# Loading q, k, v and the weights through GpSimd's DMA queue, with x turned on TensorE for three of four batches

## The chip, the cores and the metric

The program runs on one core of a Trainium2 chip. The metric is the device time of one execution, in microseconds (us); smaller is better. The engines are TensorE (PE: matmuls; PEld: its weight loads), VectorE (DVE), ScalarE (ACT), GpSimd (POOL) and SyncE (SP, which here only issues DMAs). [...]

## The reference

Two blocks follow one another. The first is attention over q, k and v of 4 batches, 8 heads, 768 positions and head size 64, where a query sees the first 4 keys (the sinks) and the 128 keys up to itself. Its output, x, goes into a gated block with a spatial product along the sequence.

```python
scores = scale * np.matmul(q, k.transpose(0, 1, 3, 2))
keep = is_sink | in_window
a = softmax(np.where(keep, scores, -1e9))
x = np.matmul(a, v)                      # [4, 768, 512]
u, v = split(gelu_tanh(x @ w_in))        # each [4, 768, 512]
v_n = (v - mean) / np.sqrt(var + 1e-06) * g_ln
v_s = np.einsum('ts,bsd->btd', w_sg, v_n) + b_sg[None, :, None]
return x + (u * v_s) @ w_out
```

(The lines are shortened: softmax, split and gelu_tanh stand for what the reference writes out.) Inputs and output are float32; the kernel multiplies in bfloat16.

## The kernel before

The work is cut into steps of some instructions each, with a name and indices: batch, then head pair or group. The string STEPS (lines 15 to 64) lists all of them in order, and the program is made by walking that list. This one order fixes the order on every engine's queue; semaphores between engines are added where a tile is shared. Nothing else decides the order. HOLDS adds two waits by hand: LQ.1.0 and LG wait until the load LWS has landed. PSUM is held in two rings: `sc` of 2 tiles for scores and MLP products, `mm` of 4 tiles for all else.

For attention, per batch b and head pair p (4 pairs):

- LQ, LK, LV (lines 171 to 179) load q, k and v of one pair as float32, each 384 KB, from SP's queue. For q and k a partition takes 6 neighbouring positions, so a row in memory is 1,536 bytes; for v a row is 256 bytes.
- CQ, CK, CV (cast, line 182) turn them into bfloat16 on GpSimd; q and k of a pair are laid side by side, so that 128 columns hold both heads.
- TQ and TK (line 266) turn q and k on TensorE, six 128x128 transposes each. EQ (DVE, line 276) and EK (ACT, line 281) evict them to qT and kT.
- KS and SK (lines 287, 296) form the sink keys and their scores; SX takes their exponential. LC (line 209) loads the sink rows of v for all batches from ACT's queue, and VSM (lines 252, 253) spreads them.
- QK (line 310) makes scores for a group g of two key tiles, EX (ACT, line 318) the exponential, MK the band mask: on DVE by a product (line 325) or on GpSimd by two selects (lines 329, 333).
- AV (lines 350, 356, 360) multiplies with v, NR (DVE, lines 369, 370) normalises into x.

For the MLP of a batch, x has to be turned: for batch 0 by XT and XE on TensorE and ACT (lines 378, 384), for batches 1 to 3 by XD, two DMA transposes from SP's queue (line 388). MV (line 399) and MU (line 446) are the two halves of x @ w_in, GV and GU (ACT) their GELUs. BN (DVE, lines 411, 412) takes mean and variance, RS (GpSimd) the reciprocal root, Z the normalised rows. SP (line 466) is the spatial product; GT and GM (DVE, lines 471, 476) gate it; OU (line 483) multiplies with w_out; RA (line 487) adds x and ST stores. WT and WE turn w_sg once.

LW, LWS and LWO load the weights from GpSimd's queue, casting on the way. The MLP of batch b is interleaved with the attention of batch b+1 and part of b+2, so the program has an attention of batch 0 that stands nearly alone, four stages that each begin with MV, and a tail.

Of the kernel before, what the change touches and what calls it, by code (L numbers as in the profile page):

```python
# [13 lines left out]

STEPS = """
IDEN ZERO LC MASK LQ.0.0 LK.0.0 LQ.0.1 LK.0.1 VSK LQ.0.2 LK.0.2 LV.0.0 LQ.0.3 LK.0.3 CQ.0.0 LV.0.1 LV.0.2 TQ.0.0
CK.0.0 VSM.1 LV.0.3 EQ.0.0 TK.0.0 CQ.0.1 EK.0.0 VSM.3 TQ.0.1 CK.0.1 VSM.0 QK.0.0.2 QK.0.0.1 EX.0.0.2 KS.0.0 TK.0.1
EQ.0.1 CQ.0.2 SK.0.0 VSM.2 TQ.0.2 CK.0.2 EQ.0.2 SX.0.0 QK.0.0.0 MK.0.0.2 TK.0.2 EX.0.0.1 CV.0.0 EK.0.2 MK.0.0.1
EX.0.0.0 QK.0.2.2 KS.0.2 CQ.0.3 EX.0.2.2 MK.0.0.0 QK.0.2.0 LW.0 EK.0.1 QK.0.2.1 LW.1 EX.0.2.1 AV.0.0.0 KS.0.1 TQ.0.3
NR.0.0.0 EX.0.2.0 SK.0.1 MK.0.2.2 SK.0.2 MK.0.2.1 AV.0.0.1 SX.0.2 CK.0.3 MK.0.2.0 QK.0.1.0 SX.0.1 QK.0.1.1 CV.0.1  # L20
EX.0.1.0 NR.0.0.1 EQ.0.3 CV.0.2 EX.0.1.1 QK.0.1.2 CV.0.3 MK.0.1.0 TK.0.3 EX.0.1.2 XT.0.0 MK.0.1.1 LWS AV.0.2.1 EK.0.3
AV.0.2.0 XE.0.0 NR.0.2.1 MK.0.1.2 QK.0.3.2 QK.0.3.1 AV.0.1.0 EX.0.3.2 KS.0.3 NR.0.2.0 SK.0.3 LWO AV.0.1.1 EX.0.3.1
NR.0.1.0 QK.0.3.0 MK.0.3.2 XT.0.2 SX.0.3 NR.0.1.1 EX.0.3.0 MK.0.3.1 XT.0.1 XE.0.2 AV.0.3.1 MK.0.3.0 XE.0.1 NR.0.3.1
AV.0.3.0 NR.0.3.0 XT.0.3 XE.0.3 MV.0.2 MU.0.3 GV.0.2 LQ.1.0 LK.1.0 WT.3 WT.4 LV.1.0 WE.3 WT.5 LG WT.2 WE.4 GU.0.3
MV.0.0 WE.5 LQ.1.1 WE.2 LK.1.1 BN.0.2 LV.1.1 MV.0.1 GV.0.0 LQ.1.2 CQ.1.0 LK.1.2 RS.0.2 LV.1.2 BN.0.0 MU.0.0 LQ.1.3
GV.0.1 CK.1.0 LK.1.3 LV.1.3 Z.0.5 WT.1 RS.0.0 LQ.2.0 GU.0.0 TK.1.0 BN.0.1 LK.2.0 MU.0.1 EK.1.0 CV.1.0 Z.0.0 WE.1
TQ.1.0 WT.0 RS.0.1 Z.0.4 Z.0.1 LV.2.0 MU.0.2 WE.0 GU.0.1 EQ.1.0 CQ.1.1 GU.0.2 CK.1.1 Z.0.2 TQ.1.1 LQ.2.1 QK.1.0.2
Z.0.3 QK.1.0.0 LK.2.1 CV.1.1 EX.1.0.2 EQ.1.1 TK.1.1 SP.0.0.3 LV.2.1 CQ.1.2 SP.0.1.2 GT.0.0.3 LQ.2.2 EK.1.1 CK.1.2
GM.0.0.3 SP.0.0.1 EX.1.0.0 GT.0.1.2 MK.1.0.2 LK.2.2 GM.0.1.2 QK.1.1.0 GT.0.0.1 SP.0.1.0 CV.1.2 EX.1.1.0 MK.1.0.0
QK.1.1.1 LV.2.2 GM.0.0.1 CQ.1.3 SP.0.1.1 GT.0.1.0 EX.1.1.1 MK.1.1.0 LQ.2.3 CK.1.3 TQ.1.3 GT.0.1.1 TK.1.2 TQ.1.2  # L30
MK.1.1.1 LK.2.3 EQ.1.3 EK.1.2 TK.1.3 QK.1.0.1 EK.1.3 QK.1.1.2 EQ.1.2 SP.0.0.0 CV.1.3 EX.1.0.1 GM.0.1.1 CQ.2.0 LV.2.3
SP.0.1.3 KS.1.0 EX.1.1.2 MK.1.0.1 LQ.3.0 GT.0.0.0 QK.1.2.1 SK.1.0 GM.0.1.0 EX.1.2.1 GM.0.0.0 MK.1.1.2 GT.0.1.3
QK.1.3.1 SX.1.0 TQ.2.0 GM.0.1.3 MK.1.2.1 QK.1.3.2 EX.1.3.1 EQ.2.0 AV.1.0.0 OU.0.3 NR.1.0.0 CQ.2.1 AV.1.0.1 RA.0.3
MK.1.3.1 TQ.2.1 EX.1.3.2 NR.1.0.1 AV.1.1.1 ST.0.3 QK.1.2.2 CK.2.1 EQ.2.1 QK.1.3.0 EX.1.2.2 AV.1.1.0 OU.0.4 MK.1.3.2
NR.1.1.1 EX.1.3.0 NR.1.1.0 TK.2.1 CQ.2.2 AV.1.3.1 EK.2.1 RA.0.4 QK.1.2.0 CK.2.0 TQ.2.2 NR.1.3.1 EX.1.2.0 ST.0.4
QK.2.1.1 MK.1.2.2 LK.3.0 TK.2.0 EQ.2.2 SP.0.0.2 EX.2.1.1 CK.2.2 MK.1.2.0 EK.2.0 AV.1.2.1 GT.0.0.2 MK.2.1.1 TK.2.2
# [503 lines left out]
```

The softmax here doesn't subtract the row's maximum and nothing guards it: scores larger than these inputs give would overflow.

## Time and profile before

| What | Value |
|---|---|
| Median of 8 runs | 173.12 us (172.12 to 174.8) |
| The profiled execution | 172.6 us |
| Its span, first to last instruction | 170.6 us |
| PE busy | 148.7 us (87%) |
| DVE busy | 138.5 us (81%) |
| ACT busy | 102.0 us (60%) |
| POOL busy | 96.1 us (56%) |
| DMA on SP's queue | 27.93 MB, 61.9% of 16 engines |
| DMA on GpSimd's queue | 2.75 MB, 9.8% of 16 engines |
| Read from HBM | 24.81 MB |

The span runs from the first instruction to the last; the execution's own time has 2.0 us more. Busy time is a mean over stages with different limits, so it is read stage by stage. A group of instructions is shown with its line in the kernel, its engine, what it writes and reads, how often it occurs, its busy time and the mean length of one in ns. In rows of the timeline, the bracket at the end holds the idle time before an instruction and what ended it.

### The profile page before, as it was taken

The page shows a single profiled execution, that of the slowest core. Times are in us where ns is not written, and L with a number is a line of the kernel's source. Part 1 is how long each engine was busy: PE and PEld are TensorE (multiplying, and loading weights), DVE is VectorE, ACT ScalarE, POOL GpSimd, SP SyncE. Part 2 cuts the span into 40 slices and gives each one's busy share as a digit, 9 for nine tenths or more (in the row PEclk, how much of TensorE's full clock was granted, in tenths as well). Part 3 has the DMA queues.
Part 4 walks back from the last instruction along what each step waited for, and adds up shares of the span by engine and source line. Part 5 has one row for each costly group of instructions (what it writes and reads, how often), then busy time and mean ns, then how long its engine had stood idle before and what let it go on. Part 6 is the DMA issues. An engine that isn't in the chain of part 4 may idle for free.

```text
span 170.6 us, 3610 instructions
## 1 busy us (share of the span) xinstructions
PE 148.7 (87%) x1375; PEld 89.0 (52%) x1388; DVE 138.5 (81%) x290; ACT 102.0 (60%) x119; POOL 96.1 (56%) x158
## 2 busy tenths in 40 slices
PE   0356789599999899889999999999999999999970
PEld 0233566365665566645576565544666744566530
DVE  6189599439989999999998899839889994959962
ACT  0415979674995768956659975864897006860000
POOL 7679776014999999999599578144306400510000
PEclk9999999999999999999999999999999999999999
DMA  5999989999999999979999101970100374110144
GB/s 165 301 322 246 200 134 174 212 291 223 318 305 299 297 297 295 322 149 230 329 320 295 32 4 26 221 248 0 61 4 0 69 174 179 73 61 0 37 153 184
DMA packets 49617, 30.94 MB, mean 181 GB/s; under 512 B 35904, under 2 KB 46400, under 8 KB 49600
## 3 DMA queue, kind: packets, MB, share of 16 engines
q1 hardware_dynamic: 47072, 27.93, 61.9%
q0 software_dynamic: 2368, 2.75, 9.8%
...
q10 hardware_dynamic: 160, 0.03, 0.1%
HBM read 24.81 MB, written 6.29 MB: 182 GB/s over the span
## 4 chain that ended last, share of the span: by engine, by line
PE 62%; DVE 20%; ACT 5%; POOL 3%; DMA 3%; issue 3%; ACTq 2%; DVEq 0%
PE mm L466 15%; PE mm L483 11%; PE sc L446 10%; PE sc L399 10%; PE sc L310 5%; DMA vs<-in_v_dram 3%; DVE x_sb L370 3%; PE mm L266 3%; DVE qT L276 3%; ACT P L318 3%; DVE gtmp L471 3%; PE mm L350 3%; DVE P L325 3%; DVE wsg_gated L476 2%; PE mm L356 2%
## 5 line engine op out<-in xcount | busy, mean ns | idle before, releaser
L318 ACT ACTIVATE P<-sc 128x1024 bf16<-128x1024 f32 (+1 forms) x48 | 43.9, 959 | 11.5 <-PE sc L310 10.1
L466 PE MATMUL mm<-wsgT,z 128*128 128x384 bf16 x192 | 34.0, 326 | 0.0
L329 POOL TENSOR_SCALAR_AFFINE_SELECT P<-P 128x512 bf16<-128x512 bf16 x28 | 20.2, 720 | 17.2 <-ACT P L318 13.0
L466 PEld LDWEIGHTS <-z 128*128 128x128 bf16 x192 | 18.0, 98 | 12.1 <-issue 1.2
L483 PE MATMUL mm<-w_out_sb,wsg_gated 128*128 128x512 bf16 x88 | 22.3, 379 | 1.5 <-DVE wsg_gated L476 1.1
L399 PE MATMUL sc<-w_in_sb,xT 128*128 128x512 bf16 x93 | 22.2, 379 | 0.4 <-ACT xT L384 0.2
L446 PE MATMUL sc<-xT,w_in_sb 128*128 128x384 bf16 x128 | 22.4, 326 | 0.0
L471 DVE SCALAR_TENSOR_TENSOR gtmp<-mm,g_sb,b_bc 128x384 bf16<-128x384 f32 x32 | 19.3, 611 | 3.6 <-PE mm L466 3.5
L487 DVE TENSOR_TENSOR ot<-mm,x_sb 128x512 f32<-128x512 f32 x24 | 16.1, 684 | 5.4 <-PE mm L483 5.3
L310 PE MATMUL sc<-qT,kT 64*128 64x256 bf16 x192 | 16.8, 285 | 4.1 <-DVE qT L276 1.7
L182 POOL TENSOR_SCALAR q<-q 128x768 bf16<-128x768 f32 x16 | 14.3, 893 | 9.3 <-DMA q<-in_q_dram 9.3
L404 ACT ACTIVATE vt<-sc 128x1024 f32<-128x1024 f32 x12 | 12.3, 1025 | 11.7 <-PE sc L399 11.7
L350 PE MATMUL mm<-v_sb,P 128*128 128x65 bf16 x192 | 17.3, 197 | 1.8 <-DVE P L325 1.6
L370 DVE TENSOR_TENSOR x_sb<-mm,rcp 128x384 bf16<-128x384 f32 x32 | 17.8, 558 | 1.1
L411 DVE BATCH_NORM_STATS2 st<-vt 128x6 f32<-128x512 f32 x24 | 16.2, 676 | 2.5 <-ACT vt L404 2.5
L350 PEld LDWEIGHTS <-P 128*128 128x128 bf16 x192 | 14.7, 100 | 6.1 <-DVE P L325 2.1
L325 DVE TENSOR_TENSOR P<-P,mask 128x1024 bf16<-128x1024 bf16 x20 | 16.5, 831 | 1.4 <-ACT P L318 1.3
L446 PEld LDWEIGHTS <-w_in_sb 128*128 128x128 bf16 x128 | 12.4, 98 | 8.4
L281 ACT COPY kT<-mm 128x768 bf16<-128x768 bf16 x16 | 12.9, 803 | 5.9 <-PE mm L266 5.9
L356 PE MATMUL mm<-v_sb,P 128*128 128x65 bf16 x160 | 16.3, 197 | 0.0
L182 POOL TENSOR_SCALAR v_sb<-v 128x768 bf16<-128x768 f32 x16 | 14.9, 937 | 1.7 <-DMA v<-in_v_dram 1.6
L476 DVE TENSOR_TENSOR wsg_gated<-gtmp,uT 128x384 bf16<-128x384 bf16 x32 | 15.1, 483 | 0.8
...
## 6 DMA issues: line engine op xcount, KB each, us to landing
...
```

The source lines that it names most:

```text
L182: return nc.gpsimd.tensor_scalar(out=dst, in0=src, scalar1=1.0, scalar2=1.0, op0=ALU.mult, op1=ALU.mult)
L310: nc.tensor.matmul(sc[:, hl, 256 * jl:256 * jl + n], kT[b, p][rows, 128 * j:128 * (j + 1)], qT[b, p][rows, 128 * j:128 * j + n], start=Tru ...
L318: nc.scalar.activation(out=pt[:, :, 0:w], in_=sc_ring[b, p, g][:, :, 0:w], func=AF.Exp, scale=scale)
L325: nc.vector.tensor_mul(pt[:, :, 0:w], pt[:, :, 0:w], m.unsqueeze(1).to_broadcast([128, 2, w]))
L329: nc.gpsimd.affine_select(out=p4[:, :, :, 0:128], in_=p4[:, :, :, 0:128], compare_op=ALU.is_ge, fill=0.0, base=0, pattern=[[0, 2], [0, 2], ...
L350: nc.tensor.matmul(av[:, il, hl, :], P[b, p, i // 2][:, hl, 256 * (i % 2):256 * (i % 2) + 128], vb[:, h, i, :], start=first, stop=False)
L370: nc.vector.tensor_mul(xs[:, 3 * half:3 * half + 3, 128 * p:128 * (p + 1)].rearrange("p t (h d) -> p t h d", h=2), av[:, :, :, 0:Dh], rcp. ...
L399: nc.tensor.matmul(hp[:, jl, :], xT[b][:, j, c, :], w_in_sb[:, c, d_half:2 * d_half], start=(c == 0), stop=(c == KD - 1))
L446: nc.tensor.matmul(hp[:, hf, 0:NH], w_in_sb[:, c, 128 * dc:128 * (dc + 1)], xT[b][:, 3 * hf:3 * hf + 3, c, :], start=(c == 0), stop=(c == ...
L466: nc.tensor.matmul(ps[:, 0:NH], z[b][:, si, 128 * dc:128 * (dc + 1)], wsgT[:, si, NH * hf:NH * (hf + 1)], start=(si == 0), stop=(si == NT ...
L471: nc.vector.scalar_tensor_tensor(out=gtmp.new((b, hf, dc)), in0=mm_ring["g", b, hf, dc][:, 0:NH], scalar=g_sb[:, dc:dc + 1], in1=b_bc[:, N ...
L483: nc.tensor.matmul(ps, gatedT[:, (2 * b + hf) % 3, dc, 128 * tl:128 * (tl + 1)], w_out_sb[:, dc, :], start=(dc == 0), stop=(dc == KU - 1))
```

## The change

- **Loads.** q and k come through GpSimd's queue, which casts them, straight into the bfloat16 tiles q16 and k16: 2 heads at a time for batch 0, 4 heads for the others. These tiles now keep each head's positions together. v comes through the same queue, uncast and pair by pair. Only q and k of the first pair come from SP's queue, in float32. The wait of LQ.1.0 for LWS is gone. DT is empty, so the branches for it are not taken.
- **Casts.** Of q and k, the first pair alone is cast, on DVE. A letter at the end of a step names the engine: CV runs 6 times on DVE, 3 on ACT, 7 on GpSimd.
- **Transposes.** TQ and TK have twelve transposes of 64 columns, one for each head and tile; head 0 of a pair is written to the lower, head 1 to the upper half of the partitions.
- **Evictions.** EQ runs 10 times on ACT and 6 on DVE; EK 8 and 8.
- **x.** XT and XE turn x of batches 0, 1 and 2 (XE 6 times on ACT, 6 on DVE); batch 3 keeps XD.
- **Sinks.** Sink rows have a stride of 16 per head. The sink scores of batches 1 to 3 are four matmuls, each to its own 32 partitions. LC is issued from SP.
- **Masks and gating.** 25 of the 48 masks run on DVE (20 before), 23 on GpSimd (28 before); GM runs 17 times on DVE and 15 on GpSimd (32 on DVE before).
- **Statistics.** RS runs twice a batch, for four rows and for two, with the power alone on GpSimd; the sum and the product around it are on DVE (BN, NM).
- **Constants.** The memsets move from GpSimd to DVE (FILL, MASK0).
- **HM.n** puts n matmuls of a constant by a constant (128x512) in front of the next PSUM tile's first writer, into that tile. There are 31, all ahead of the first MV.
- **Order.** STEPS is a new list.

```diff
--- before.py
+++ after.py
 STEPS = """
-IDEN ZERO LC MASK LQ.0.0 LK.0.0 LQ.0.1 LK.0.1 VSK LQ.0.2 LK.0.2 LV.0.0 LQ.0.3 LK.0.3 CQ.0.0 LV.0.1 LV.0.2 TQ.0.0
-CK.0.0 VSM.1 LV.0.3 EQ.0.0 TK.0.0 CQ.0.1 EK.0.0 VSM.3 TQ.0.1 CK.0.1 VSM.0 QK.0.0.2 QK.0.0.1 EX.0.0.2 KS.0.0 TK.0.1
...
+ZERO LQ.0.0 IDEN LK.0.0 LQ.0.1 FILL LK.0.1 LC VSK MASK LV.0.0 MASK0 CQ.0.0.D LQ.0.2 HM.7 TQ.0.0 LK.0.2 EQ.0.0.A HM.2
+TQ.0.1 LV.0.1 CK.0.0.D EQ.0.1.D HM.2 TK.0.0 LQ.0.3 EK.0.0.A TK.0.1 VSM.0 LK.0.3 EK.0.1.A QK.0.0.1 LV.0.2 QK.0.0.2
+KS.0.0 VSM.2 EX.0.0.1 SK.0.0 LV.0.3 KS.0.1 CV.0.0.D HM.2 SK.0.1 TQ.0.2 VSM.1 LW.0 EX.0.0.2 HM.1 TK.0.2 VSM.3 QK.0.1.0
+LW.1 SX.0.0 QK.0.1.1 MK.0.0.2.D EX.0.1.0 CV.0.1.D LWS EK.0.2.D EX.0.1.1 HM.4 QK.0.1.2 TQ.0.3 MK.0.0.1.P EQ.0.2.D
+EX.0.1.2 QK.0.0.0 MK.0.1.1.P EX.0.0.0 HM.1 QK.0.2.0 SX.0.1 KS.0.2 LWO HM.1 QK.0.2.2 CV.0.2.D EX.0.2.0 AV.0.0.1
...
+NR.0.3.0 LV.1.3 HM.2 XT.0.2 NR.0.3.1 XE.0.2.A LQ.2.0 HM.3 XT.0.3 LK.2.0 LG WT.3 XE.0.3.D WT.5 WT.4 WE.3 MV.0.0 WE.5
+WE.4 MV.0.1 GV.0.0 WT.2 WT.1 WE.2 WT.0 GV.0.1 MV.0.2 BN.0.0 BN.0.1 TQ.1.0 GV.0.2 TQ.1.1 MU.0.2 EQ.1.1.A BN.0.2
+EQ.1.0.A RS.0.1 MU.0.0 GU.0.2 CV.1.0.P MU.0.3 NM.0.1 GU.0.0 WE.1 RS.0.2 WE.0 Z.0.1.A LV.2.0 Z.0.3.D TK.1.1 Z.0.2.A
+CV.1.1.D TK.1.0 TQ.1.2 NM.0.2 LV.2.1 EK.1.1.A EK.1.0.D MU.0.1 Z.0.0.A EQ.1.2.D LQ.2.1 GU.0.3 TQ.1.3 Z.0.4.D LK.2.1
+TK.1.3 GU.0.1 Z.0.5.D TK.1.2 QK.1.0.0 EK.1.3.D EQ.1.3.A SP.0.0.0 CV.1.2.P EX.1.0.0 EK.1.2.D SP.0.0.1 LV.2.2 GT.0.0.0
...
+SP.3.0.1 GT.3.1.3 GM.3.1.3.P SP.3.1.0 GT.3.0.1 GM.3.0.1.D SP.3.1.1 GT.3.1.0 GM.3.1.0.D OU.3.1 GT.3.1.1 OU.3.2
+GM.3.1.1.D RA.3.1 OU.3.4 RA.3.2 ST.3.1 OU.3.5 ST.3.2 RA.3.4 OU.3.3 ST.3.4 OU.3.0 RA.3.5 RA.3.0 ST.3.5 ST.3.0 RA.3.3
+ST.3.3
...
-HOLDS = "LQ.1.0<LWS LG<LWS"
+HOLDS = "LG<LWS"
+
+
+DT = ()
...
-    q16 = Ring("q16", 3, [128, NT, 2, Dh], BF16)
-    k16 = Ring("k16", 3, [128, NT, 2, Dh], BF16)
+    q16 = Ring("q16", 3, [128, 4, NT, Dh], BF16)
+    k16 = Ring("k16", 3, [128, 4, NT, Dh], BF16)
...
+    def HM(n):
+        pre[0] = n
+
+    def fresh(ring, key):
+        t = ring.new(key)
+        for _ in range(pre[0]):
+            nc.tensor.matmul(t if ring is mm_ring else t[:, 0, :], iden, ks_sink[1][:, 0:512], start=True, stop=True)
+        pre[0] = 0
+        return t
...
-    def LQ(b, p):
-        return nc.sync.dma_start(out=q32.new((b, p)), in_=q[b, 2 * p:2 * p + 2].rearrange("h (p t) d -> p h (t d)", p=128))
-
-    def LK(b, p):
-        return nc.sync.dma_start(out=k32.new((b, p)), in_=k[b, 2 * p:2 * p + 2].rearrange("h (p t) d -> p h (t d)", p=128))
+    def load(ring, src, b, i):
+        n = 2 if b == 0 else 4
+        hs = slice(n * i, n * i + n)
+        dst = ring.get((b, n * i // 4))[:, n * i % 4:n * i % 4 + n].rearrange("p h t d -> p h (t d)")
+        return nc.gpsimd.dma_start(out=dst, in_=src[b, hs].rearrange("h (p t) d -> p h (t d)", p=128))
+
+    def rows(eng, ring, src, b, p):
+        return eng.dma_start(out=ring.new((b, p)).rearrange("p h t d -> p (h t) d"),
+                                 in_=src[b, 2 * p:2 * p + 2].rearrange("h (t p) d -> p (h t) d", p=128))
+
+    def first(name, src):
+        return nc.sync.dma_start(out=v32.new(name).rearrange("p h t d -> p h (t d)"),
+                                 in_=src[0, 0:2].rearrange("h (p t) d -> p h (t d)", p=128))
+
+    def LQ(b, i):
+        if (b, i) == (0, 0):
+            return first("q", q)
+        return rows(nc.sync, q32, q, b, i) if b in DT else load(q16, q, b, i)
+
+    def LK(b, i):
+        if (b, i) == (0, 0):
+            return first("k", k)
+        return rows(nc.sync, k32, k, b, i) if b in DT else load(k16, k, b, i)
 
     def LV(b, p):
-        return nc.sync.dma_start(out=v32.new((b, p)).rearrange("p h t d -> p (h t) d"),
-                                 in_=v[b, 2 * p:2 * p + 2].rearrange("h (t p) d -> p (h t) d", p=128))
-
-    def cast(dst, src):
+        return rows(nc.sync if b in DT else nc.gpsimd, v32, v, b, p)
+
+    def copy(e, dst, src):
+        if e == "A":
+            return nc.scalar.copy(dst, src)
+        if e == "D":
+            return nc.vector.tensor_copy(dst, src)
         return nc.gpsimd.tensor_scalar(out=dst, in0=src, scalar1=1.0, scalar2=1.0,
                                        op0=ALU.mult, op1=ALU.mult)
 
-    def CQ(b, p):
-        return cast(q16.new((b, p)).rearrange("p t h d -> p h t d"),
-                    q32[b, p].rearrange("p h (t d) -> p h t d", d=Dh))
-
-    def CK(b, p):
-        return cast(k16.new((b, p)).rearrange("p t h d -> p h t d"),
-                    k32[b, p].rearrange("p h (t d) -> p h t d", d=Dh))
-
-    def CV(b, p):
-        return cast(v_sb[b % 2][:, 2 * p:2 * p + 2, :, 0:Dh], v32[b, p])
+    def CQ(b, p, e):
+        if b == 0:
+            return copy(e, q16.get((0, 0))[:, 0:2], v32["q"])
+        return copy(e, qn.new((b, p)).rearrange("p t h d -> p h t d"), q32[b, p])
+
+    def CK(b, p, e):
+        if b == 0:
+            return copy(e, k16.get((0, 0))[:, 0:2], v32["k"])
+        return copy(e, kn.new((b, p)).rearrange("p t h d -> p h t d"), k32[b, p])
+
+    def CV(b, p, e):
+        return copy(e, v_sb[b % 2][:, 2 * p:2 * p + 2, :, 0:Dh], v32[b, p])
...
     def LC():
-        for s in range(n_sink):
-            nc.scalar.dma_start(out=vs32[s:NS:n_sink, :, :], in_=v[:, :, s, :].rearrange("b h d -> h b d"))
+        for i in range(n_sink):
+            nc.sync.dma_start(out=vs32[i:128:16, :, :], in_=v[:, :, i, :].rearrange("b h d -> h b d"))
...
     def transposes(name, ring, b, p):
-        src = ring[b, p].rearrange("p t h d -> p t (h d)")
-        mm_ring.new((name, b, p))
+        src = ring[b, p // 2]
+        fresh(mm_ring, (name, b, p))
         ps = psb((name, b, p))
         for t in range(NT):
-            nc.tensor.transpose(ps[:, t, :], src[:, t, :], iden)
+            for hl in range(2):
+                nc.tensor.transpose(ps[64 * hl:64 * hl + 64, t, :], src[:, 2 * (p % 2) + hl, t, :], iden)
...
-    def EQ(b, p):
-        dst = qT.new((b, p))
-        nc.vector.tensor_copy(dst.rearrange("p (i t) -> p i t", t=NT),
-                              psb(("q", b, p)).rearrange("p t i -> p i t"))
-
-    def EK(b, p):
-        dst = kT.new((b, p))
-        nc.scalar.copy(dst.rearrange("p (i t) -> p i t", t=NT),
-                       psb(("k", b, p)).rearrange("p t i -> p i t"))
+    def turned(dst, name, src, b, p, e):
+        if b in DT:
+            return nc.sync.dma_start_transpose(out=dst.new((b, p)).rearrange("p (t i) -> p t i", t=NT),
+                                               in_=src[b, p].rearrange("p t h d -> p (t h d)"))
+        copy(e, dst.new((b, p)).rearrange("p (i t) -> p i t", t=NT), psb((name, b, p)).rearrange("p t i -> p i t"))
+
+    def EQ(b, p, e=None):
+        return turned(qT, "q", qn, b, p, e)
+
+    def EK(b, p, e=None):
+        return turned(kT, "k", kn, b, p, e)
...
     def SK(b, p0):
-        prs = range(HP) if b else (p0,)
-        ps = mm_ring.new(("s", b, p0))
-        for n, p in enumerate(prs):
-            nc.tensor.matmul(ps, ks_sink[b % 2][:, 128 * p:128 * (p + 1)], qT[b, p][:, 256:768],
-                             start=(n == 0), stop=(n == len(prs) - 1))
+        ps = fresh(mm_ring, ("s", b, p0))
+        ks = ks_sink[b % 2]
+        if b == 0:
+            nc.tensor.matmul(ps, ks[:, 128 * p0:128 * (p0 + 1)], qT[b, p0][:, 256:768], start=True, stop=True)
+            return
+        for p in range(HP):
+            c0 = (128 + ks_w) * p
+            nc.tensor.matmul(ps[ks_w * p:ks_w * (p + 1), :], ks[:, c0:c0 + ks_w], qT[b, p][:, 256:768],
+                             start=True, stop=True)
...
-    def MK(b, p, g):
+    def MK(b, p, g, e="D"):
         w = 512 if g < NG - 1 else 384
         pt = P[b, p, g]
-        if g == 0 or (b == 0 and g not in MK0):
+        if e == "D":
...
-    def XE(b, p):
-        dst = xT.get(b)[:, :, p, :]
-        if (b, p) in XED:
-            return nc.vector.tensor_copy(dst, psb(("x", b, p)))
-        return nc.scalar.copy(dst, psb(("x", b, p)))
+    def XE(b, p, e):
+        copy(e, xT.get(b)[:, :, p, :], psb(("x", b, p)))
...
+        if jj:
+            nc.vector.tensor_scalar(out=rs.get(b)[:, part(jj)], in0=mv[:, part(jj), 1], scalar1=1e-6,
+                                    scalar2=None, op0=ALU.add)
...
+        r = rs[b][:, part(jj)]
+        nc.gpsimd.tensor_tensor(r, r, neg_half[:, part(jj)], op=ALU.pow)
+
+    def NM(b, jj):
+        nc.vector.scalar_tensor_tensor(out=nmr.get(b)[:, part(jj)], in0=mvs[b][:, part(jj), 0], scalar=-1.0,
+                                       in1=rs[b][:, part(jj)], op0=ALU.mult, op1=ALU.mult)
...
-    def GM(b, hf, dc):
-        nc.vector.tensor_mul(gatedT[:, (2 * b + hf) % 3, dc, :], gtmp[b, hf, dc],
+    def GM(b, hf, dc, e):
+        (nc.vector if e == "D" else nc.gpsimd).tensor_mul(gatedT[:, (2 * b + hf) % 3, dc, :], gtmp[b, hf, dc],
```

## The prediction

> **What bounds the kernel now.** I read the page's first rows, then cut the span where the batches' value projections (MV) begin, because those divide the program into attention of batch 0, four overlapped stages and a tail. The windows answer gives each stage; columns are start:end, length, busy time of PE, PEld, DVE, ACT and POOL, clock, DMA share and GB/s.
>
> ```profile
> PE 148.7 (87%) x1375; PEld 89.0 (52%) x1388; DVE 138.5 (81%) x290; ACT 102.0 (60%) x119; POOL 96.1 (56%) x158
> DMA  5999989999999999979999101970100374110144
> ```
> ```profile
> 0.00:33.00 33.00, 19.07 (x228) 13.06 (x230) 23.55 (x48) 19.04 (x24) 22.98 (x42) 1.00 1.02 219
> 33.00:47.60 14.60, 13.78 (x113) 8.37 (x114) 10.21 (x23) 10.62 (x13) 7.17 (x13) 1.00 1.09 274
> 47.60:79.20 31.60, 29.80 (x347) 18.39 (x351) 30.71 (x59) 24.44 (x29) 31.06 (x43) 1.00 1.07 276
> 79.20:112.40 33.20, 33.04 (x322) 19.98 (x324) 30.08 (x66) 24.57 (x29) 23.55 (x38) 1.00 0.74 179
> 112.40:139.40 27.00, 26.95 (x238) 15.72 (x238) 23.05 (x53) 14.38 (x17) 8.22 (x17) 1.00 0.23 64
> 139.40:170.60 31.20, 26.05 (x139) 13.43 (x138) 20.91 (x44) 8.90 (x10) 3.08 (x8) 1.00 0.30 107
> ```
>
> TensorE (PE) is full from 79 us on; 47.6-79.2 is shared by PE, VectorE (DVE) and GpSimd (POOL), all above 94%; DMA is full until about 94 us. A busy PE includes pipeline latency, so I priced its work by the chain's back-to-back rows: 216 ns for a 512-column matmul, 163 for 384, 56 for a transpose. So priced, the six stages hold 11.5, 13.5, 27.5, 32.6, 26.3 and 26.0 us of PE work: real slack lies ahead of 79 us and in the tail. The start, from the timeline:
>
> ```profile
> 9.34 0.90 DVE L253 TENSOR_TENSOR v_sink<-vs,headsel 32x512 bf16<-32x512 f32 x1 [3.72 <-DMA vs<-in_v_dram]
> 10.16 0.94 DVE L276 COPY qT<-mm 128x768 bf16<-128x768 bf16 x1
> 11.69 0.81 ACT L318 ACTIVATE P<-sc 128x768 bf16<-128x768 f32 x1 [3.36 <-PE sc L310]
> ```
>
> DVE waits 3.72 us for the sink rows of v, with the q eviction queued behind; the first exponential is at 11.69. Later the q load of batch 1 is held until the w_sg load has landed, and leaves at 32.55.
>
> **The change, part by part.**
>
> **GpSimd.** It loses 32 casts of q and k, 0.89 us each (28.6), and 9 of 16 casts of v at 0.94 (8.4). It gains 34 DMA issues. The four weight issues took 0.75 to 1.00 us for 512 to 768 rows, so 18 q and k issues (256 or 512 rows) cost 0.75; a v load has 1,536 rows of 256 B, which no row shows: 0.87 if rows are free, 1.75 if proportional, 1.2 taken, as 512 to 768 rows added little. Sum 32, between 27 and 42. Five masks fewer save 6, the shorter statistics 7, the memsets 2; 15 GM products come over at about 0.9 (two inputs of 384 elements at the cast's rate). Net 96 to about 89, so its average doesn't bind. What matters is order: a DMA issue that waits for a buffer now holds masks, powers and products behind it. Here each load's buffer is freed several steps earlier by DVE or PE, so I charge no wait; if that cover fails, each one costs what the late mask costs AV, the 1.0 us of the DVE mask wait now seen at 72-73 us.
>
> **VectorE.** In batch 0 it takes over two casts of q and k and three of v, some 0.6 each (estimate: a 768-element cast took 0.83 on POOL; DVE's 1,024-element mask 0.68), two K and two x evictions. Overall: qT evictions 16 to 6 (-9.5), kT +8 (+7.6), xT +6 at 0.55 (+3.3), casts +4.8, masks 20 to 25 (+3.9), GM 32 to 17 (-7.2), statistics +3, about +6. But it should work faster in the crowded stage. The mask row there against later, and the gated product likewise:
>
> ```profile
> L325 DVE TENSOR_TENSOR P<-P,mask x6: 777/1057/1305, 52.3 to 79.0; 128x1024 bf16<-128x1024 bf16 x6
> L325 DVE TENSOR_TENSOR P<-P,mask x7: 677/681/1117, 79.0 to 131.4; 128x1024 bf16<-128x1024 bf16 x7
> L476 DVE TENSOR_TENSOR wsg_gated<-gtmp,uT x8: 343/621/974, 50.2 to 70.7; 128x384 bf16<-128x384 bf16 x8
> L476 DVE TENSOR_TENSOR wsg_gated<-gtmp,uT x24: 346/358/783, 94.6 to 163.5; 128x384 bf16<-128x384 bf16 x24
> ```
>
> Same shapes, 0.26-0.38 us more while POOL is full. POOL's work in that stage falls from 32.2 to some 20, so DVE's nominal 31 us there can shrink to 28. Against it stands "SBUF — State Buffer", section "SBUF: two separate sides": a GpSimd-issued DMA can't have its descriptors written while DVE runs a two-port operation. By the trace, issues took at most 1.00 us beside a busy DVE; by the rule, each of the 8 DVE casts could hold an issue for its 0.6, 4.8 us in all, on POOL with slack. I use the row and leave the rule to the range.
>
> **TensorE.** Eight more groups of x transposes (48 of 56 ns): 8 x 0.34 = +2.7. The sink scores of batches 1-3 go from four accumulating 216 ns matmuls to four on 32-column parts: 0.87 to some 0.35, -1.6. The q and k transposes are the large unknown: twelve of 64 columns instead of six of 128, writing the two partition halves in turn. Rows:
>
> ```profile
> 92.17 0.67 PE mm L266 x12
> 47.60 0.49 PE sc L310 x8
> ```
>
> Twelve 128-wide transposes take 0.67, so a group is 0.34. The scores (L310) are eight 256-column matmuls on the two row halves; at 109 ns each they'd need 0.87, and take 0.49: halves run in pairs. If column halves pair likewise, a group stays at 0.34. Against that speak "TensorEngine Tiling (Array Packing)", section "Restrictions" (column tiling turns fast weight loading off), and "TensorE: Matmul & The Clock Gate", section "LDWEIGHTS" (columns over 1.2 GHz): 64 columns are 53 ns, twelve in a row 0.64. No run here has a column-tiled row. By the row it adds 0, by the rule 24 x 0.30 = +7.2 us behind batch 0. I take 0.42, nearest the score pairs with something for changing mode: +1.9.
>
> The 31 constant matmuls cost 6.7 us at 216 ns, nearly all ahead of 33 us, where PE works 11.5 of 33 us; on the path only if operands come earlier than planned, each then 0.2 us. ACT gains 10 q, loses 8 k evictions, gains two x copies and three casts: +6, hidden at 60%.
>
> **DMA.** Bytes are the same but the order isn't. Four of six x transposes go (4.4 us to landing each, hidden now). q and k of batch 1 come as 4-head loads, and the step list asks for the second k of batch 1 before the first score of batch 1. Ahead of and with it in the queue: 4.7 MB of batch 0, 5.5 of weights, 3.15 of q and k, 0.8 of v, 14.1 MB. The kernel before had 9.2 MB in at 32.5 us, from 1.9: 300 GB/s. So it lands at 1.9 + 47 = 48.9; at 340 GB/s 43.4, at 275 53.
>
> **The sum, by checkpoints.** First exponential: q evicts without the sink rows, but now two pairs are transposed and three evictions stand ahead on ACT: 10.0 against 11.7. Batch 0's attention then has some 20.3 us of DVE work with 1 idle: first MV at 31.3, not 33.0 (29-34). First score of batch 1: PE has 14.1 + 0.6 of work, done at 46, then waits for the load: 49.0 against 47.6 (46-53). To the next MV: PE 26.1 + 0.6, and 1.5 idle, 28.2 against 31.6, at 77.2. Then 32.9 against 33.2 (110.1); 28.6 against 27.0 as x transposes and other work of 1.6 us fall there (138.7); tail 30.6 against 31.2, since two OU groups fill the 1.10 us in which the last OU waits for GM. Ends at 169.3, that is 1.3 below the span of 170.6. The profiled execution took 172.6, 2.0 more than its span; the median of the runs is 173.12, half a microsecond above it. So 173.1 - 1.3 = 171.8 us, 0.8% faster.
>
> **The rivals.** (1) *Loads don't gate:* at 340 GB/s batch 1 is in at 43.4 and PE goes straight on; three microseconds more are kept, and with transposes at 0.34 another 2: about 167. For it: DMA moved 334 GB/s in 5-10 us; against: 276 in the crowded stage. (2) *Column tiles run at the weight-load price* (slower than before): 0.64 a group adds 0.22 x 24 = 5.3, of which 0.9 lies under the load wait: 176.2. It decides from 0.50 a group, where the 1.3 gained is spent. For it: the two sections; against: the score pairs. (3) *GpSimd as one queue stalls:* descriptors for some 11,000 rows stand ahead of the first masks; a full queue or slower generation (1.75 for v, +9 on POOL, some 3-4 ahead of the first score of batch 1) makes loads 4 us late: 175.5. For it: POOL was full at 47-74 us; against: its earlier issues never waited. (4) *Nothing gained:* PE's later stages set the time and the early gain is lost to the load order: 173.1.
>
> **How the numbers follow.** Chances: forecast 30%, (1) 20%, (2) 27%, (3) 11%, (4) 12%. Of the forecast's 30 some 27 lie over 0.5% below (0.5%, 0.9 us, is about what a measurement of this kernel can tell from no change): faster 0.47, same 0.12 + 0.03 = 0.15, slower 0.38. The forecast's own range is 169.5-173.5. The range that leaves out 2 in 10 reaches into (1) and through (2) and (3): 166.5 to 177.5.
>
> **What would show it.** Right: first exponential near 10, first MV near 31, first score of batch 1 near 49 with PE waiting for k, mask rows near 0.7 in 48-78, a q transpose group near 0.4. Wrong: groups of 0.6 or more, POOL's v issues above 1.5, masks late behind DMA issues, or a first score of batch 1 well ahead of 47.

## The result, and the profile after

The changed kernel takes 171.87 us (median of 11 runs, 169.72 to 172.81), the kernel before 172.99 beside it (32 runs). The ratio is 0.990, with a 95% interval of 0.986 to 0.994: 0.6 to 1.4% shorter. The ratio leaves out executions over 1.5% above the fastest of the same kernel, so it is not the quotient of the two medians, and of the changed kernel's executions that it keeps, three took 169.7 to 169.8 us and the others, the profiled one among them, 171.4 to 172.2. The forecast was 171.8. The profiled execution took 171.51 us, its span 169.8; the gain of this one span is 0.8 us, the gain of the medians 1.1.

The checkpoints, read from the first instruction of each step (us from the start of the span):

| Checkpoint | Before | Forecast | After |
|---|---|---|---|
| First exponential | 11.69 | 10.0 | 11.56 |
| First MV (batch 0) | 33.0 | 31.3 | 32.3 |
| First score of batch 1 | 47.5 | 49.0 | 47.0 |
| MV of batch 1 | 79.0 | 77.2 | 76.5 |
| MV of batch 2 | 112.4 | 110.1 | 109.6 |
| MV of batch 3 | 139.3 | 138.7 | 138.9 |
| End | 170.6 | 169.3 | 169.8 |

The gain was 2.5 to 2.8 us when MV of batches 1 and 2 began. Of that, 2.4 us went again in the stage from MV of batch 2 to MV of batch 3. The total came out close to the forecast, but the path to it differs.

First the page of the changed kernel: busy times, the DMA row of the 40 slices, the packets, and the rows of the v loads and of the gated products that moved to GpSimd (busy, mean ns, idle before).

```profile
PE 156.7 (92%) x1644; PEld 91.7 (54%) x1659; DVE 139.6 (82%) x312; ACT 106.9 (63%) x127; POOL 90.2 (53%) x124
DMA  5999999999999413099992000331100295011054
DMA packets 20114, 23.49 MB, mean 138 GB/s; under 512 B 4864, under 2 KB 15360, under 8 KB 20096
L200 POOL DMA_DIRECT2D v<-in_v_dram x16 | 17.0, 1072 | 7.0 <-DVE x_sb L419 3.6
L513 POOL TENSOR_TENSOR wsg_gated<-gtmp,uT 128x384 bf16<-128x384 bf16 x15 | 14.5, 969 | 11.3 <-DVE gtmp L508 9.8
```

GpSimd is at 90.2 us (some 89 were reckoned): a v issue costs 1.07 (1.2 taken), a product 0.97 (0.9 taken). The DMA row was full to slice 22 before; now it has gaps from slice 14 on. The kernel before had 49,617 packets for the same reads from HBM.

The stages by windows (columns as before; edges at the checkpoints):

```profile
0.00:32.30 32.30, 25.84 (x322) 15.04 (x327) 24.69 (x60) 19.30 (x24) 26.89 (x42) 1.00 1.09 205
32.30:47.00 14.70, 14.65 (x172) 8.99 (x170) 11.58 (x27) 10.32 (x14) 8.62 (x11) 1.00 1.19 250
47.00:76.50 29.50, 28.43 (x392) 17.47 (x393) 27.51 (x60) 25.73 (x33) 18.57 (x27) 1.00 0.62 140
76.50:109.60 33.10, 32.92 (x392) 20.55 (x393) 29.95 (x67) 27.36 (x33) 20.07 (x28) 1.00 0.50 113
109.60:138.90 29.30, 28.82 (x243) 16.10 (x242) 25.55 (x58) 15.43 (x17) 10.48 (x13) 1.00 0.30 69
```

Of the three engines that were above 94% in the crowded stage only PE is left there: it works 28.43 of 29.50 us (96%), DVE 27.51 (93%), GpSimd 18.57 (63%). Two DVE rows of that time, by source line (min/median/max in ns):

```profile
L374 DVE TENSOR_TENSOR P<-P,mask x8: 681/683/980, 52.6 to 75.7; 128x1024 bf16<-128x1024 bf16 x7, 128x768 bf16<-128x768 bf16 x1
L513 DVE TENSOR_TENSOR wsg_gated<-gtmp,uT x6: 343/348/798, 53.1 to 68.5; 128x384 bf16<-128x384 bf16 x6
```

Before, the same mask had a median of 1,057 ns there and the product 621. From the chain of the changed kernel, transposes of q and k (L309), 12 instructions to a group, and the sink scores (L345); start, length:

```profile
51.98 0.33 PE mm L345 x4
55.34 0.79 PE mm L309 x24
98.21 1.46 PE mm L309 x48
```

Here x counts instructions, so x24 is two groups. Two take 0.79 and four 1.46, so one more group is worth (1.46 - 0.79) / 2 = 0.335 us, what a group of six 128-wide transposes took before (0.34). The sink scores of a batch fell from 0.87 (four of 216 ns) to 0.33.

Last, how the queue on GpSimd behaves, from its timeline (start, length, and in brackets the idle time ahead):

```profile
33.59 1.02 POOL L200 DMA_DIRECT2D v<-in_v_dram  x1 [1.10 <-DMA w_out_sb<-in_moe_w_out_dram]
36.59 0.76 POOL L197 DMA_DIRECT2D q<-in_q_dram  x1 [1.98 <-DMA q<-in_q_dram]
```

In this trace an issue waits until an earlier load, unrelated to its own buffer, has landed: in both rows it is the load eight issues before. The second k load of batch 1, which the forecast had gating TensorE at 48.9 us, landed at 44.7, ahead of the first score at 47.0.

### The profile page after: what moved, and what is told of

It is laid out like the page before. It is cut to its first block, busy times and chain, and to the rows that moved or that the text cites. A ratio compares the mean times of both kernels' runs of the same rounds, so it can differ in the third digit from the quotient of the medians.

```text
span 169.8 us, 4085 instructions
## 1 busy us (share of the span) xinstructions
PE 156.7 (92%) x1644; PEld 91.7 (54%) x1659; DVE 139.6 (82%) x312; ACT 106.9 (63%) x127; POOL 90.2 (53%) x124
## 4 chain that ended last, share of the span: by engine, by line
PE 70%; DVE 18%; ACT 4%; issue 2%; POOL 2%; DVEq 1%; POOLq 0%
PE mm L503 15%; PE sc L443 11%; PE mm L520 11%; PE sc L483 9%; PE mm L309 6%; PE sc L359 5%; PE mm L399 3%; DVE x_sb L419 3%; DVE P L374 3%; ACT P L367 3%; PE mm L185 3%; DVE st L456 2%; PE mm L405 2%; PE mm L427 2%; DVE kT L224 2%
## 5 line engine op out<-in xcount | busy, mean ns | idle before, releaser
L503 PE MATMUL mm<-wsgT,z 128*128 128x384 bf16 x192 | 34.6, 327 | 0.4 <-DVE z L476 0.4
L378 POOL TENSOR_SCALAR_AFFINE_SELECT P<-P 128x512 bf16<-128x512 bf16 x23 | 16.1, 701 | 21.0 <-ACT P L367 21.0
L520 PE MATMUL mm<-w_out_sb,wsg_gated 128*128 128x512 bf16 x88 | 22.8, 379 | 0.4
L200 POOL DMA_DIRECT2D v<-in_v_dram x16 | 17.0, 1072 | 7.0 <-DVE x_sb L419 3.6
L513 POOL TENSOR_TENSOR wsg_gated<-gtmp,uT 128x384 bf16<-128x384 bf16 x15 | 14.5, 969 | 11.3 <-DVE gtmp L508 9.8
L374 DVE TENSOR_TENSOR P<-P,mask 128x1024 bf16<-128x1024 bf16 (+1 forms) x25 | 18.0, 732 | 0.0
L399 PE MATMUL mm<-v_sb,P 128*128 128x65 bf16 x192 | 16.4, 194 | 1.1 <-DVE P L374 0.6
L464 POOL TENSOR_TENSOR rs<-rs,neg_half 128x4 f32<-128x4 f32 (+1 forms) x8 | 7.1, 892 | 19.0 <-DVE rs L459 18.6
L359 PE MATMUL sc<-qT,kT 64*128 64x256 bf16 x192 | 15.4, 264 | 0.9 <-DVE kT L224 0.4
L488 ACT ACTIVATE uT<-sc 128x768 bf16<-128x768 f32 x16 | 12.9, 811 | 5.2 <-PE sc L483 5.2
L405 PE MATMUL mm<-v_sb,P 128*128 128x65 bf16 x160 | 15.6, 194 | 0.0
```

What stands on the lines that cost most here:

```text
L359: nc.tensor.matmul(sc[:, hl, 256 * jl:256 * jl + n], kT[b, p][rows, 128 * j:128 * (j + 1)], qT[b, p][rows, 128 * j:128 * j + n], start=Tru ...
L374: nc.vector.tensor_mul(pt[:, :, 0:w], pt[:, :, 0:w], m.unsqueeze(1).to_broadcast([128, 2, w]))
L399: nc.tensor.matmul(av[:, il, hl, :], P[b, p, i // 2][:, hl, 256 * (i % 2):256 * (i % 2) + 128], vb[:, h, i, :], start=first, stop=False)
L405: nc.tensor.matmul(av[:, il, hl, :], P[b, p, j // 2][:, hl, 256 * (j % 2) + 128:256 * (j % 2) + 256], vb[:, h, j, :], start=False, stop=False)
L503: nc.tensor.matmul(ps[:, 0:NH], z[b][:, si, 128 * dc:128 * (dc + 1)], wsgT[:, si, NH * hf:NH * (hf + 1)], start=(si == 0), stop=(si == NT ...
L520: nc.tensor.matmul(ps, gatedT[:, (2 * b + hf) % 3, dc, 128 * tl:128 * (tl + 1)], w_out_sb[:, dc, :], start=(dc == 0), stop=(dc == KU - 1))
```

## The experiments

### Are column halves really paired?

```diff
-        for t in range(NT):
-            for hl in range(2):
+        for hl in range(2):
+            for t in range(NT):
                 nc.tensor.transpose(ps[64 * hl:64 * hl + 64, t, :], ...)
```

> Edit: in each q and k transpose group the six transposes of head 0 come first, then the six of head 1, so neighbours write the same column half. My theory (the two column halves run in pairs, which is why a group costs some 0.37 us): a group goes to about 0.67 us, 24 groups behind batch 0 add up to 7 us of TensorE work, and the kernel comes to 175.5-178.5 us, slower than the kernel before. Rival (groups are cheap for another reason, short weight loads): groups stay below 0.45 and the time stays at 171.9.

Measured: 174.79 us, ratio 1.008 (1.005 to 1.011). Its chain, and below it the single group of the changed kernel (the four are shown above):

```profile
13.20 0.59 PE mm L309 x12
100.62 1.60 PE mm L309 x48
```

```profile
12.60 0.46 PE mm L309 x12
```

A single group takes 0.59 where it took 0.46, so it loses 0.13. Four in a row take 1.60, only 0.14 more than 1.46. In the trace the instructions of the second half of one group start between those of the first half of the next, 26 to 30 ns apart. So the pairing is real and worth something. But the two halves move ahead on their own, and the order inside a group is exposed only where a run of groups ends. All pieces of L309 on the chain sum to 12.26 us, against 9.70: 2.6 of the 3.4 us by which the spans differ; most of the rest is a chance meeting on DVE that is told below. The expected 0.3 a group was too much by half or more, and the time stayed just below the expected 175.5 to 178.5.

### What are the constant matmuls worth?

First all 31 left out, then all but the first seven.

```diff
     def HM(n):
-        pre[0] = n
+        pre[0] = 0
```

> Edit: no constant matmuls at all. My theory (two of the pairs stand on the chain ahead of the first exponential, 0.97 us each, and several later ones delay a score): first exponential near 9.8 instead of 11.56, first MV 1-2 us earlier, the end 0.5-1.5 us earlier, about 171. Rival (they raise TensorE's rate early, which pays for them): transposes and scores stay at twice the spacing up to about 20 us and the first MV isn't earlier; 172 to 173.

```diff
-... HM.2 TQ.0.1 ... HM.2 TK.0.0 ... HM.4 QK.0.1.2 ...   (every HM but HM.7)
+... TQ.0.1 ... TK.0.0 ... QK.0.1.2 ...
```

> The changed kernel with only the first seven constant matmuls (ahead of the first transposes of q); the other 24 are gone. My theory: those 24 lie in gaps or add up to 1 us on the path to the first exponential, and do nothing for the clock once real work is dense: ratio to the kernel before 0.985 to 0.990, that is 0 to 0.8 us shorter than the changed kernel; first exponential at 9.7 to 11.5, first value projection at 31.5 to 32.3. Rival: they keep TensorE's clock up in the gaps before 33 us, and without them the time goes to that of the kernel without any: 173.0 (ratio 0.995) or more, with rows of half rate after 12 us.

Measured: without any 173.04 us, ratio 0.995 (0.991 to 1.000); with the first seven 172.52, ratio 0.992 (0.984 to 1.000). Both intervals overlap that of the changed kernel, 0.986 to 0.994. PE's rows of the windows in the run without any, then in the changed kernel:

```profile
12.00:18.00 6.00, 3.19 (x52) 0.93 1.12 238
18.00:26.00 8.00, 6.60 (x120) 0.84 1.20 207
```

```profile
12.00:18.00 6.00, 4.98 (x65) 1.00 1.13 232
18.00:26.00 8.00, 6.43 (x110) 1.00 1.20 207
```

Without them the granted clock dropped in this stretch, with them it didn't. The same shows between executions: the mean clock of the whole span was below 0.99 in 8 of 12 without any and in 5 of 6 with the first seven, against 1 of 12 in the changed kernel. Yet that profiled execution was 0.9 us shorter than the changed kernel's (168.9). It had its first exponential at 9.72 and its first MV at 31.45, 0.8 earlier. So the constants hold the clock, but what that gives in time and what they take on the path can't be told apart by these runs. It stays open.

### Is it worth moving casts off GpSimd?

```diff
-        return copy(e, v_sb[b % 2][:, 2 * p:2 * p + 2, :, 0:Dh], v32[b, p])
+        return copy("P", v_sb[b % 2][:, 2 * p:2 * p + 2, :, 0:Dh], v32[b, p])
```

> Edit: all sixteen casts of v on GpSimd, where the changed kernel has nine of them on DVE and ACT. My theory (GpSimd has slack; DVE is relieved by 4.5 us and ACT by 2.4, but GpSimd's tensor work holds DVE's): between -0.5 and +1.5 us, 171.5-173.5. Rival (a GpSimd queue with DMA issues in it binds): the casts delay issues and masks, over 174.

Measured: 174.46 us, ratio 1.011 (1.007 to 1.015), 2.6 us above the changed kernel. From its windows:

```profile
47.39:77.84 30.45, 28.79 (x392) 17.51 (x393) 28.20 (x59) 24.49 (x31) 21.74 (x31) 1.00 0.61 137
77.84:112.39 34.55, 33.70 (x392) 20.74 (x392) 31.52 (x66) 26.91 (x32) 21.97 (x30) 1.00 0.48 107
```

The two stages lengthen from 29.45 to 30.45 and from 33.1 to 34.55; the others stay within 0.4. The time is above 174, as the rival had it, but not by its mechanism: GpSimd is only at 71% and 64% in these stages, and TensorE waits for a mask or product of GpSimd 0.5 us at the longest. DVE is what changes: it is busy 142.1 us, with six casts (4.5 us) fewer than in the 139.6 of the changed kernel. Two of its eight masks in the crowded stage took 1,304 and 1,117 ns (at most 980 in the changed kernel). Of the second stage 0.9 us is a meeting with GpSimd that is told further below.

### What is the one queue worth?

The v loads go to SP's queue, all else stays on GpSimd's:

```diff
-        return rows(nc.sync if b in DT else nc.gpsimd, v32, v, b, p)
+        return rows(nc.sync, v32, v, b, p)
```

> Edit: all loads of v issued from SP's queue; q, k and the weights stay on GpSimd's. GpSimd has 16 issues of 1.07 us less. My theory (loads land ahead of need, GpSimd isn't the limit): 171.5-172.5, no difference. Rival (one GpSimd queue stalls the kernel): faster by over 1 us, below 171.

Measured: 190.35 us, ratio 1.101 (1.097 to 1.106); neither expectation had that. From its waits (total, times, longest), and its packets:

```profile
POOL v_sb L225 <- DMA v<-in_v_dram: 22.2, 2, 19.5
DVE v_sb L224 <- DMA v<-in_v_dram: 19.1, 3, 8.8
```

```profile
DMA packets 43155, 23.50 MB, mean 125 GB/s; under 512 B 29440, under 2 KB 39936, under 8 KB 43136
```

The v loads of batch 0 landed at 13.8, 23.4, 34.6 and 39.0 us (10.4 to 19.9 on GpSimd's queue), though issued early. The weights, issued on the other queue from 7.5 us, overtook them, and the first MV came at 51.3. The difference in packets under 512 B is 24,576, which is 16 loads of 1,536 rows. So on SP's queue each row of v is a packet; on GpSimd's those rows don't appear as such.

Is it the small rows alone, or the company? The first weight load is made to wait for the last v load of batch 0:

```diff
+        return rows(nc.sync, v32, v, b, p)
...
-HOLDS = "LG<LWS"
+HOLDS = "LG<LWS LW.0<LV.0.3"
```

> As the run with the v loads on SP's queue (190.35 us), but the first weight load waits for the last v load of batch 0 to have landed, so that no weight load shares the DMA engines with them. My theory (the two queues share the engines and the small rows of v lose): the v loads of batch 0 land by 20 us instead of 23.4 to 38.95, the first value projection is back at 32 to 36 us, and the time at 173 to 178. Rival (v's rows of 256 B are slow on SP's queue whatever else runs): v of batch 0 still lands after 28 us, and the time stays above 183.

Measured: 177.53 us, ratio 1.028 (1.021 to 1.034). v of batch 0 now lands at 14.3, 16.6, 18.2 and 20.0 us, as on the one queue. So it was the company of the weights: beside them the queue with a packet per small row lost. The first MV is at 38.6, later than expected. Here GpSimd itself stands in the added wait, ahead of its masks and of the weights, so this time is no price of v on SP's queue alone:

```profile
POOL w_in_sb L243 <- DMA v<-in_v_dram: 12.8, 1, 12.8
```

### Could x of batches 1 and 2 stay on DMA?

```diff
-... NR.1.3.1 ... XT.1.0 ... XE.1.0.A ... XT.2.1 ...       (XT and XE of batches 1 and 2)
+... NR.1.3.1 XD.1.1 ... NR.1.3.0 XD.1.0 ... XD.2.0 ... XD.2.1 ...
```

> The changed kernel with the attention output x of batches 1 and 2 also turned by DMA, each half issued behind its last normalisation (batch 0 stays on TensorE, batch 3 stays on DMA). This takes eight transpose groups (8 x 0.34 = 2.7 us) off TensorE and eight evictions off DVE and ScalarE. My theory: in the changed kernel the last normalisation of batch 1 ends at 73.6 us and the value projection starts at 76.5; a DMA transpose took 4.4 us to land in the kernel before, so x comes at 78.0 and TensorE, whose other work there ends near 75, idles some 2 to 3 us; for batch 2 (105.6, 109.75) some 1 us. Net 0 to 1.5 us longer than the changed kernel: 172 to 173.5 (ratio to the kernel before 0.995 to 1.003). Rival: the transposes on TensorE are pure cost on the engine that bounds, and without them the kernel is 2.5 us shorter: 169.3 (ratio 0.979).

Measured: 194.73 us, ratio 1.124 (1.117 to 1.131). Waits of PE, and the first MV of batch 1:

```profile
PE sc L442 <- DMA xT<-x_sb: 19.0, 1, 19.0
```

```profile
95.48 3.59 PE L442 MATMUL sc<-w_in_sb,xT 128*128 128x512 bf16 x8 [19.04 <-DMA xT<-x_sb]
```

Nine loads (the last v of batch 2 and all of batch 3) are issued on GpSimd's queue from 70 to 81 us and land by 97.9. The transposes of batch 1 were issued on SP's at 72.8 and 76.0, and the projection that waits for them could begin only at 95.5. Those of batch 2, issued at 125.6 and 127.2 with no load in flight, landed in 3.7 and 4.0 us. Even that stage, from MV of batch 1 to MV of batch 2, is 35.4 us instead of 33.1. The direction was foreseen, the size not by far. With this order of loads, then, the transposes on TensorE are no addition beside the one queue but its condition: the DMA transposes were through only when the bulk nearly was. That doesn't hold for every transfer on the other queue: in the changed kernel the load of b_sg (384 KB, 3,072 bytes to a partition) was issued from SP at 30.5 us, amid loads on GpSimd's queue, and landed 6.6 us later. Whether small packets make the difference is not shown.

### Is the gain only the early sink wait?

The kernel before, with its wait for the sink rows moved:

```diff
-CK.0.0 VSM.1 LV.0.3 EQ.0.0 TK.0.0 ...
+CK.0.0 LV.0.3 EQ.0.0 TK.0.0 VSM.1 ...
```

> The kernel before with one step moved: the scaling of the sink rows of v for batch 1, whose load lands at 9.3 us, goes behind the evictions and transposes of the first pair, so DVE no longer waits 3.72 us ahead of the first q eviction. My theory: the first exponential comes about 1.5 us earlier (10.2 instead of 11.69), but DVE's later work and the late v loads of batch 0 take most of it: 0 to 1 us less in all, 172.1 to 173.1 (ratio 0.994 to 1.000). Rival: the start is the path, and what the first exponential gains is carried through to the end: 1.5 to 2.5 us less, 170.6 to 171.6 (ratio 0.986 to 0.991), and the changed kernel's gain would be this alone.

Measured: 172.24 us, ratio 0.997 (0.992 to 1.002). The first exponential comes at 9.37, 2.3 us earlier; the first MV 0.9 earlier (32.05), MV of batches 1 to 3 at 78.1, 111.4 and 138.4, the end at 169.7, 0.9 earlier. More than half of the early gain is spent before the first MV. The medians give 0.5 us, which the interval doesn't tell from nothing; the rival's ratio of at most 0.991 lies just outside it.

### Where did the stage of batch 2 lose time?

Three variants of the gated products, all on the changed kernel:

```diff
-GM.2.0.3.P GM.2.0.2.P GM.2.0.1.P GM.2.1.1.P GM.2.1.3.P GM.2.1.2.P
+GM.2.0.3.D GM.2.0.2.D GM.2.0.1.D GM.2.1.1.D GM.2.1.3.D GM.2.1.2.D
```

> The changed kernel with the gated products of batch 2 all on DVE (six of eight come back from GpSimd). It tests where the stage from batch 2's value projection to batch 3's lost time: 29.3 us against 27.0 in the kernel before, with DVE on the chain at 126.8 to 133.8 us. My theory (GpSimd's two-input products slow DVE's: a product of 128x384 took DVE 1.07 us beside GpSimd's own and 0.35 alone): DVE gets five products of 0.35 more in the stage but loses the collisions, and the stage shortens to 28.0 to 28.8 us; the time falls by 0.5 to 1 us (ratio to the kernel before 0.984 to 0.988). Rival (DVE simply carries too much there): 5 x 0.35 = 1.7 us more on DVE, the stage at 30 to 31 us, ratio 0.996 to 1.000.

```diff
-GM.b.h.c.P      (all 15)
+GM.b.h.c.D
```

> The changed kernel with all 32 gated products on DVE, as in the kernel before. My theory: in batch 0's and 1's products GpSimd takes work off a full DVE, so that moving 15 back costs more there than it gives in the stage of batch 2: ratio to the kernel before 0.990 to 0.997, 0 to 1.2 us longer than the changed kernel, with the stage from 47 to 76.5 us longer by 0.5 to 1. Rival: a product on GpSimd saves DVE 0.35 us and costs it as much by slowing it, and gives the chain 0.6 us more latency: then all on DVE is 0.5 to 1.5 us shorter (ratio 0.981 to 0.987).

```diff
-GM.2.0.0.D GM.2.1.0.D MK.3.3.2.D
+GM.2.0.0.P GM.2.1.0.P MK.3.3.2.P
```

> The opposite of the first: in the changed kernel two more gated products of batch 2 (the two that DVE computed near 128.0 and 131.3 us) and one mask of batch 3 (0.99 us at 131.56) go from DVE to GpSimd. My theory: DVE loses 2.4 us of work in that stretch, but GpSimd's products take 0.97 to 1.4 us each and the output projection waits for them: the stage stays at 29 to 30 us, the time within 0.5 us of the changed kernel (ratio 0.987 to 0.993). Rival (DVE's load is the bound there): the stage shortens by 1 to 2 us to 27.3 to 28.3, ratio 0.979 to 0.985.

Measured, with stages cut at the first MV of each batch:

| Kernel | Ratio (interval) | First score of batch 1 to MV 1 | MV 1 to MV 2 | MV 2 to MV 3 |
|---|---|---|---|---|
| Changed | 0.990 (0.986 to 0.994) | 29.45 | 33.1 | 29.3 |
| Batch 2 on DVE | 0.999 (0.996 to 1.001) | 29.44 | 34.05 | 29.0 |
| All on DVE | 0.995 (0.992 to 0.998) | 29.45 | 33.5 | 29.0 |
| More on GpSimd | 1.001 (0.999 to 1.003) | 29.44 | 34.05 | 29.6 |

In the stage in question moving products either way changes 0.3 us, in the direction of my theory but at half its size or less. The crowded stage isn't touched at all: the ratio of the second came out as expected, its reason did not. The ratios are worse by 0.5 to 1.1%. The profiled spans are longer by 0.6, 0.6 and 1.5 us, which is less than that; the rest lies between executions and isn't explained. Within the spans the loss is in the stage from MV 1 to MV 2, whose code is the same in the first, the third and the changed kernel. One DVE step there differs: four products of 128x8 that fill ks_sink. The changed kernel, then the one with batch 2 on DVE:

```profile
105.64 1.29 DVE L332 TENSOR_TENSOR ks_sink<-kT,halfsel 128x8 bf16<-128x8 bf16 x4
```

```profile
105.65 2.23 DVE L332 TENSOR_TENSOR ks_sink<-kT,halfsel 128x8 bf16<-128x8 bf16 x4
```

Both reach the step at the same time and leave it 0.94 us apart, which is the difference of the stage, 34.05 against 33.11. Beside it GpSimd, in the kernel with batch 2 on DVE, and the durations of DVE's line there:

```profile
105.67 0.64 POOL L378 TENSOR_SCALAR_AFFINE_SELECT P<-P 128x512 bf16<-128x512 bf16 x1
106.26 0.64 POOL L382 TENSOR_SCALAR_AFFINE_SELECT P<-P 128x512 bf16<-128x512 bf16 x1
106.86 0.91 POOL L513 TENSOR_TENSOR wsg_gated<-gtmp,uT 128x384 bf16<-128x384 bf16 x1
```

```profile
L332 DVE TENSOR_TENSOR ks_sink<-kT,halfsel x16: 149/154/958, 11.0 to 107.7; 128x8 bf16<-128x8 bf16 x16
```

Eight elements in a partition need 154 ns. Three of the four took 681, 666 and 958, and each ended within 0.05 us of the end of the GpSimd instruction beside it. In the profiles of nine variants of the changed kernel (all but the one with all gated products on DVE and the one below) the four together took 2.1 to 2.4 us there and the stage 34.05 us or more; in the changed one they took 1.3, and with all gated products on DVE 0.4 (whose stage of 33.5 is thus not explained by them). The Trainium skill, "SBUF — State Buffer", section "SBUF: two separate sides", says what fits this: a DVE operation with two inputs in SBUF and a GpSimd operation that reads SBUF exclude one another for a whole instruction, and the one that starts first goes first. By sharing in proportion, a 154 ns operation might take 0.3 (an estimate: twice its time); the rows show it waiting to the end.

To test it, those products go to GpSimd for batches 1 to 3:

```diff
-            nc.vector.tensor_mul(
+            (nc.gpsimd if b else nc.vector).tensor_mul(
                 ks_sink[b % 2][...], ...)
```

> The changed kernel with the small products that put k's sink rows into ks_sink (128x8, four a batch, 154 ns each on DVE alone) moved from DVE to GpSimd for batches 1 to 3. In the runs so far, where they met GpSimd's masks near 106 us on DVE, each of them ended with a GpSimd instruction (0.60 to 0.96 us for 24 columns' work), and the four took 1.3 us in the changed kernel, 2.2 us in two others and 0.3 us in a fourth; the stage from batch 1's value projection to batch 2's took 33.1, 34.05, 34.05 and 33.5 us. My theory: the loss comes from DVE being held while GpSimd computes, so on GpSimd itself it is gone: DVE has no such wait near 106 us, the stage takes 32.6 to 33.1 us, and the ratio to the kernel before is 0.985 to 0.990. Rival: what GpSimd takes over makes the sink scores late (they stand behind two masks and a product on its queue): the stage takes 33.5 to 34.5 us, ratio 0.992 to 0.998.

Measured: 171.55 us, ratio 0.990 (0.985 to 0.994). The stage is 33.0 us (32.6 to 33.1 expected), DVE has no such wait there, and PE's weight loads wait for these products 0.4 us. On GpSimd the four took:

```profile
105.99 1.23 POOL L332 TENSOR_TENSOR ks_sink<-kT,halfsel 128x8 bf16<-128x8 bf16 x4
```

One of them took 752 ns, beside a DVE mask of 0.70 that ran from 106.14: now it is GpSimd that is held, and the four take 1.23 us, hardly less than the 1.29 on DVE. In time it equals the changed kernel, so no version beyond that one is shown to be faster.

Most of the 2.4 us lost from MV of batch 2 to MV of batch 3 is work that moved. There the kernel before has four groups of the output projection (OU, four matmuls each), the changed one six. Eight more of 216 ns are 1.7 us, which the stage ahead no longer has. The remaining 0.7 fits DVE, which is on the chain from 126.8 to 133.8 us; no run isolates it.

## Why the prediction was right or wrong

**What bounds.** Right: PE works at least 96% of each stage from 47 to 138.9 us, and the crowded stage gave the gain. From the first score of batch 1 to the next MV it went from 31.5 to 29.45 us. The forecast said 28.2. Of the missing 1.2, 1.0 is two DVE steps that write z, with k evictions and PE's spatial product waiting behind them. The changed kernel, then the one without constants:

```profile
46.38 2.35 DVE L476 TENSOR_SCALAR z<-vt,rs,nmr 128x512 bf16<-128x512 f32 x2
```

```profile
45.53 1.37 DVE L476 TENSOR_SCALAR z<-vt,rs,nmr 128x512 bf16<-128x512 f32 x2
```

Both times GpSimd issues two loads and casts v beside them, yet they took 1.38 and 1.05 us in one and 0.63 and 0.83 in the other, whose stage was 28.5 us. In the two kernels with v on SP's queue GpSimd had done its cast before and issued nothing there; they took 0.53 each and the stage 28.4. So this is a second such meeting, in a stage whose code was the same.

**DVE gets faster where GpSimd does less.** Right in size (1,057 to 683 ns), and the run with the casts back on GpSimd, 2.6 us slower with more time on DVE, supports it, though the median of its masks there stayed at 684. GpSimd's work there was misread as 32.2 us (the row has 31.06) and fell to 18.57, not 20. The forecast took it for slowing; the later rows point to waiting for whole GpSimd instructions. So it depends on where two instructions meet, not only on GpSimd's load.

**The page on descriptors.** The same section of the Trainium skill, "SBUF: two separate sides" in "SBUF — State Buffer", says that DVE can hold back the descriptors of a GpSimd-issued DMA. The 16 v issues took 1.02 to 1.32 us, median 1.05. A delay of 0.6 per cast is not seen, and using the row was right.

**Column tiles.** The row was right: 0.335 a group, not 0.42 and not 0.64. The term was 0.08 x 24 = 1.9 us too large, and rival (2) fell. "TensorEngine Tiling (Array Packing)", section "Restrictions and Gotchas", takes fast weight loading from column tiles: a weight load of 64 columns took 110 ns (median), one of 128 before 98, and that cost nothing visible here.

**The load gate.** This step failed. The rate was too low: the same 14.1 MB were in at 44.7 us, from 1.9, so 329 GB/s and not 300. The first score of batch 1 didn't wait for them: the chain is on DVE from 36.28 to 50.47 us, with no load in it. I had said that the bytes are the same and carried the old rate over. But the old rate was measured with a packet for every 256 B of v; that this made it lower is likely and not shown. Rival (1) was right in its mechanism (43.4 reckoned); its 167 didn't follow, since TensorE reached that point at 47.0, not 46, and lost time behind it.

**The start.** The first exponential came at 11.56 in the profile, not at 10.0. TensorE ran at half rate there until 11.2 us, which the reckoning left out: its constant matmuls started 427 ns apart and later 216, though the row of the granted clock reads 1.00 throughout. Two of the constant pairs, 0.97 us each, stand on the chain, of which I had allowed 0.2 a matmul. In the run with the sink products on GpSimd, which is the same up to there, the full rate came by 6.6 us and the first exponential at 10.04; why is open. Yet that run's first MV was no earlier (32.6 against 32.3): an early start can be lost again before 32 us.

**GpSimd as one queue.** The sum was right (90.2 against 89), and rival (3) didn't happen: its issues wait for earlier loads, but nothing urgent stood behind. I had looked for the danger in the wrong place. What hurt in these runs is small rows or DMA transposes on a second queue beside the full one.

**XT.** I counted 2.7 us of work on TensorE as its price and never asked what x by DMA would cost beside the new queue. For batches 1 and 2 it would have cost 22.9 us (194.73 against 171.87).

**The later stages.** I had put 1.6 us more in the stage of batch 2; it was 2.4, 1.7 of it from eight OU matmuls. The tail was 30.9 (30.6 reckoned).

That the total came within 0.1 us is luck. The errors cancel: 1.0 too little up to the first MV, 3.0 too much from there to the first score of batch 1, 1.2 too little in the stage behind it and 1.2 too little in all after that. What was foreseen is the kind of gain, in the crowded stage, and that it would be small.
